# Weight rounding: the sign bit is taken from ScalarE's scaled copy in PSUM instead of from the loaded words

## Chip, cores and metric

The kernel runs on one core of a Trainium2 chip. The metric is the time of one execution on the device in microseconds (us), the median of several runs; lower is better. Times inside an execution come from the hardware profiler's trace of one run.

## What is computed

The reference is a recurrent attention block (RWKV5) followed by a gated feed-forward block (SwiGLU). For 4 batches, 8 heads, 768 time steps and a head dimension of 48 it computes

```
for t in range(S):
    y[t]  = r[t] @ (state + (u * k[t]) v[t]^T)
    state = w * state + k[t] v[t]^T
x   = y as (3072, 384)
g   = x @ w_gate                      # (384, 1536)
out = (silu(g) * (x @ w_val)) @ w_out # (1536, 384)
```

The inputs r, k, v, w and u are 32-bit floats. The three weight matrices arrive as **64-bit floats**: they are drawn as 32-bit numbers and multiplied by a 64-bit scale. [...] the kernel has to round each weight to 32 bits on the chip, and it does so with integer operations. That rounding is where the change lies.

## The kernel before

**Tiling.** Time is cut in chunks of 128 steps, so there are 24 items (6 chunks times 4 batches). For each item the kernel loads r, k and v, scales them by powers of w, transposes them, forms a masked 128x128 score matrix for each head, multiplies it with v, adds what the carried state gives, and updates the state. The result lies transposed in a ring buffer `xT`, ready as an operand of the feed-forward block. That block takes items in pairs: `gate_value` (from L444) multiplies `xT` with 128 columns of w_gate and of w_val into one PSUM bank (L450), ScalarE takes the sigmoid (L456), and VectorE makes two products (L457, L458); L458 is the last reader of the bank. There are two such banks. Later pairs of items run through a faster matrix scheme (L627 and around) whose sums of weights GpSimd makes.

**Weights.** The weights are cut in 18 chunks, each 128 partitions x 768 64-bit words: 6 of w_gate, 6 of w_val (alternating), then 6 of w_out. SyncE's queue issues the loads (L152) into a ring of three slots, `w_bits`, 768 KB each. A word has a low and an upper half of 32 bits. The steps for one chunk `n`, in the order in which `round_act` (from L201) issues them:

1. `round_high(n, 0, 0)`, ScalarE, L173: the upper words of the first half of the chunk (384 of each partition), read as 32-bit floats, are multiplied by 2^-112 into a PSUM tile `w_mag`. The scale turns the exponent of the 64-bit format into that of the 32-bit one, three places too far to the right.
2. `round_low(n)`, ScalarE, L179: the low words, read as unsigned integers and scaled by 2^-29, are rounded to an integer and put in an SBUF tile `w_low` (two slots).
3. `round_dve(n, 0)`, VectorE: L188 takes the sign bit into the weight tile (`wg`, `wv` or `wo`), L189 shifts `w_mag` left by three places and joins it to that sign.
4. `round_high(n, 1, 1)` and `round_dve(n, 1)`: the same for the second half, with `w_mag` in another bank.
5. The load of a further chunk.

In a later turn GpSimd adds `w_low` to the weight tile (`round_pool`, L218; for the first two chunks in halves, L199). The PSUM tile of each half has one buffer only, so the next chunk's L173 of that half waits until L189 has read the last one. Each w_low slot is free again when GpSimd's addition has read it.

**Order.** The schedule is written by hand: every engine executes its instructions in the order in which the program issues them, and semaphores make it wait for the other engines. `gaps` (from L703) and the table `EARLY` put the rounding of three chunks into each step of the attention loop, between its transposes (L343), scores (L381, copied under a mask by VectorE in L386), outputs (L411) and state updates (L426, L438), and pieces of the feed-forward block. ScalarE also makes diagonal matrices (L322) and copies transposed tiles out of PSUM (L347); GpSimd also scales k and r (L301, L304) and makes the products for the diagonal (L230, L231), which VectorE sums (L236). The loads of k, r and v (L115, L121) stand in the same SyncE queue as those of the weights.

Of the kernel before, what the change touches and what calls it, by code (L numbers as in the profile page):

```python
# [9 lines left out]
FP32 = mybir.dt.float32  # L10
INT32 = mybir.dt.int32
UINT32 = mybir.dt.uint32
AF = mybir.ActivationFunctionType
ALU = mybir.AluOpType
# [8 lines left out]
def fast(  # L23
# [44 lines left out]
    dve, pool, act, pe, sp = nc.vector, nc.gpsimd, nc.scalar, nc.tensor, nc.sync  # L68
# [70 lines left out]
    bits, mags, lows = {}, {}, {}  # L139
# [21 lines left out]
    def halves(x, n):  # L161

        c = chunks[n][1].shape[1]
        x = x.rearrange("p (c f) -> p c f", c=c)
        f = x.shape[2]
        return [x[:, :, 0 : f // 2], x[:, :, f // 2 : f]] if c == 3 else [x[:, 0:1], x[:, 1:2]]

    def round_high(n, half, bank):
        hi = halves(bits[n][:, :, 1], n)[half]
        ps, tag = ((ps_w, "w_mag"), (ps_o, "o"))[bank]  # L170
        mag = ps.tile([P, WN // 2], INT32, name="w_mag", tag=tag)
        mags[n, half] = mag[:].rearrange("p (c f) -> p c f", c=hi.shape[1])
        act.activation(  # L173
            mags[n, half].bitcast(FP32), hi.bitcast(FP32), AF.Abs, scale=float(2.0**-112)
        )

    def round_low(n):
# [3 lines left out]
        )  # L181

    def round_dve(n, half):
        hi = halves(bits[n][:, :, 1], n)[half]
        f = hi.shape[2]
        dst = chunks[n][1].bitcast(INT32)
        dst = dst[:, :, half * f : half * f + f] if hi.shape[1] == 3 else dst[:, half : half + 1]
        dve.tensor_scalar(dst, hi, -(1 << 31), None, ALU.bitwise_and)  # L188
        dve.scalar_tensor_tensor(  # L189
            dst, mags.pop((n, half)), 3, dst, ALU.logical_shift_left, ALU.bitwise_or  # L190
        )

    def add_low(n, half):

# [6 lines left out]
    def round_act(next_load=1):  # L201
        n = next_chunk("act")
        if n is not None:
            round_high(n, 0, 0)
            round_low(n)
            round_dve(n, 0)
            round_high(n, 1, 1)
            round_dve(n, 1)
            del bits[n]
            for _ in range(next_load):  # L210
                load_weights()
# [67 lines left out]
    for l in range(7):  # L279
        n = 1 << l  # L280
# [463 lines left out]
    own_sum(1)  # L744
    diagonal(1)
    round_high(0, 0, 0)
    round_low(0)
    flush()
    round_dve(0, 0)
    scores(1)  # L750
    warm(2)
# [514 lines left out]
```

## Time and profile before

| | |
|---|---|
| time, median of 3 runs | 629.39 us (628.95 to 630.25) |
| profiled run: span | 627.9 us |
| TensorE matmul busy | 611.4 us (97%) |
| VectorE busy | 366.8 us (58%) |
| GpSimd busy | 300.1 us (48%) |
| ScalarE busy | 239.5 us (38%) |
| L188, 36 instructions, from 15.4 to 104.4 us | 28.0 us |
| L189, 36 instructions | 20.1 us |
| L173, 36 instructions | 18.9 us |
| L179, 18 instructions | 16.5 us |

How to read the views that follow: a group of instructions is named by its source line, engine and operation, with "output<-inputs" by the names of the program's tiles and their shapes (partitions x elements). After the bar come the busy time in us and the mean duration in ns; after a second bar the time that the engine sat idle just before these instructions, with the instructions that ended most of that idle time ("<-"). A line of the timeline has the start in us, the duration in us (from the first start to the last end where several are merged, "x8"), the instruction, and in brackets an idle time ahead of it. PE is TensorE, DVE is VectorE, ACT is ScalarE, POOL is GpSimd and SP is SyncE. Busy time of TensorE is modelled from pipelined matmuls, so its share of 97% is an upper figure; what counts for this case is where its instructions do not follow one another at once.

### The profile page before, as it was taken

Reading aid. Unit: us, or ns where it says so; the run is one execution under the profiler, and the core shown is the slowest. Engines: PE = TensorE matmul, PEld = TensorE weight load, DVE = VectorE, ACT = ScalarE, POOL = GpSimd, SP = SyncE. Lnnn points to the kernel's source line nnn. Section 1 sums busy time; section 2 is a strip of 40 time slices with the busy share of each in tenths; the row PEclk is TensorE's granted clock in tenths of the full one; section 3 lists DMA queues with packets and bytes.
Section 4 is the critical chain, followed back from the end, with each engine's and each line's share of the span. In section 5 each row is a group of like instructions: output and inputs, shape, how many; then the busy total and the mean of one; then the engine's idle time right before and its main releaser. Section 6 shows DMA issues by size and latency. Waiting matters only on the chain.

```text
span 627.9 us, 13037 instructions
## 1 busy us (share of the span) xinstructions
PE 611.4 (97%) x5040; PEld 550.5 (88%) x5040; DVE 366.8 (58%) x751; ACT 239.5 (38%) x647; POOL 300.1 (48%) x350
## 2 busy tenths in 40 slices
PE   8799999999999999999999999999999999999996
PEld 7588778899888899988899888899988899988896
DVE  6889999465556563466566355665345453355460
ACT  3368777321353512245330435432253321233310
POOL 5789778946648413563543635441433211443110
PEclk9999999999999999999999999999999999999999
DMA  8979873244341203322222402121000000000001
GB/s 191 246 169 243 219 242 94 40 72 80 73 69 24 45 12 66 76 47 45 40 37 57 92 12 37 25 42 41 27 2 1 1 1 26 27 0 1 1 2 55
DMA packets 138007, 40.47 MB, mean 64 GB/s; under 512 B 128592, under 2 KB 131792, under 8 KB 137936
## 3 DMA queue, kind: packets, MB, share of 16 engines
q1 hardware_dynamic: 134480, 34.82, 26.5%
q10 hardware_dynamic: 3456, 4.72, 2.1%
q8 instruction: 42, 0.69, 0.5%
q14 instruction: 29, 0.24, 0.1%
HBM read 28.51 MB, written 4.72 MB: 53 GB/s over the span
## 4 chain that ended last, share of the span: by engine, by line
PE 86%; DVE 7%; ACT 2%; DMA 2%; issue 1%; POOL 0%; DVEq 0%; ACTq 0%; POOLq 0%
PE c_b L627 25%; PE c_a L627 21%; PE o_f L521 13%; PE o_a L521 8%; PE o_b L521 6%; PE y_ps L411 5%; PE gv L450 4%; PE s_ps L381 3%; DVE At L386 1%; PE warm L265 1%; DMA hats<-in_r_dram 1%; DMA w_bits<-in_moe_w_out_dram 1%; DVE wg L188 1%; DVE wo L188 1%; PE u_ps L426 1%
## 5 line engine op out<-in xcount | busy, mean ns | idle before, releaser
L611 POOL TENSOR_TENSOR hT<-hT,u 128x256 f32<-128x256 f32 x60 | 46.9, 782 | 149.0 <-DVE hT L610 121.8
L634 ACT COPY u<-c_a 128x256 f32<-128x256 f32 x120 | 44.5, 371 | 85.8 <-PE c_a L627 83.5
L627 PE MATMUL c_a<-t,wv 128*128 128x256 f32 x240 | 72.0, 382 | 0.1
L627 PE MATMUL c_b<-xT,wg 128*128 128x256 f32 x240 | 71.6, 380 | 0.0
L607 ACT ACTIVATE sg<-hT 128x256 f32<-128x256 f32 x120 | 50.1, 417 | 52.5 <-DVE hT L636 33.8
L322 ACT ACTIVATE At<-ident,du 128x128 f32<-128x128 f32 x176 | 62.1, 398 | 16.2 <-DVE du L236 7.3
L627 PE MATMUL c_b<-xT,s 128*128 128x256 f32 x240 | 61.6, 379 | 0.0
L641 DVE TENSOR_TENSOR u<-u,c_b 128x256 f32<-128x256 f32 x60 | 25.1, 418 | 60.5 <-PE c_b L627 55.4
L627 PEld LDWEIGHTS c_b<-xT,s 128*128 128x128 f32 x240 | 45.2, 190 | 6.6 <-DVE u L641 0.2
L627 PEld LDWEIGHTS c_a<-t,wv 128*128 128x128 f32 x240 | 44.9, 190 | 6.9 <-ACT u L634 1.1
L627 PEld LDWEIGHTS c_b<-xT,wg 128*128 128x128 f32 x240 | 45.3, 190 | 6.0
L636 DVE TENSOR_TENSOR hT<-p,c_b 128x256 f32<-128x256 f32 x60 | 25.1, 419 | 41.6 <-PE c_b L627 38.6
L587 POOL TENSOR_TENSOR s<-wv,wg 128x256 f32<-128x256 f32 x24 | 17.6, 733 | 65.5 <-PE o_f L521 50.8
L386 DVE COPY_PREDICATED At<-mask,s_ps 128x512 f32<-128x512 int32 x48 | 32.9, 741 | 19.9 <-PE s_ps L381 12.4
L450 PE MATMUL gv<-xT,wg 128*128 128x256 f32 x144 | 36.9, 392 | 3.1 <-DVE hT L458 2.5
L304 POOL TENSOR_TENSOR hats<-r_ld,rscale 128x384 f32<-128x384 f32 x20 | 20.9, 1045 | 36.1 <-DMA v_ld<-in_v_dram 19.0
L639 DVE TENSOR_TENSOR hT<-hT,c_a 128x256 f32<-128x256 f32 x60 | 25.3, 421 | 19.8 <-PE c_a L627 18.4
L643 DVE TENSOR_TENSOR hT<-u,c_b 128x256 f32<-128x256 f32 x60 | 25.2, 421 | 19.8 <-PE c_b L627 19.6
L627 PE MATMUL c_b<-t,s 128*128 128x256 f32 x120 | 36.2, 383 | 0.3 <-DVE hT L636 0.3
L411 PE MATMUL y_ps<-At,v_ld 128*32 128x128 f32 x768 | 34.9, 273 | 1.4 <-DVE At L386 1.4
L627 PE MATMUL c_b<-xT,wv 128*128 128x256 f32 x120 | 35.9, 381 | 0.0
L627 PE MATMUL c_a<-t,s 128*128 128x256 f32 x120 | 35.8, 380 | 0.0
(135 smaller groups left out, 1394.6 us busy)
## 6 DMA issues: line engine op xcount, KB each, us to landing
hats<-hats SPq DMA_DIRECT2D x192, 32.0 KB, 2.0
w_bits<-in_moe_w_gate_dram SPq DMA_DIRECT2D x6, 768.0 KB, 6.5
v_ld<-in_v_dram SPq DMA_DIRECT2D x48, 96.0 KB, 3.4
w_bits<-in_moe_w_val_dram SPq DMA_DIRECT2D x6, 768.0 KB, 5.9
w_bits<-in_moe_w_out_dram SPq DMA_DIRECT2D x6, 768.0 KB, 6.0
out_dram<-o_sb ACTq DMA_DIRECT2D x24, 192.0 KB, 1.9
k_ld<-in_k_dram SPq DMA_DIRECT2D x20, 192.0 KB, 3.1
r_ld<-in_r_dram SPq DMA_DIRECT2D x20, 192.0 KB, 3.9
```

Of the source, the lines that this page charges most:

```text
L322: lambda h=h: act.activation(At[i % 2][:, h, :], ident[:], AF.Identity, scale=du[:, h : h + 1])
L386: dve.copy_predicated(At[i % 2][:].rearrange("p (a e) t -> p a e t", e=2)[:, :, e], mask[:].bitcast(INT32).unsqueeze(1).to_broadcast([P, H ...
L411: pe.matmul(ps[32 * q : 32 * q + 32, cc, :], *x, start=start, stop=stop, skip_group_check=True,)
L450: pe.matmul(gv[:, o, :].rearrange("p (i t) -> p i t", i=2), wt[:, c, P * f : P * (f + 1)], xT[:, 2 * g % NX : 2 * g % NX + 2, c, :], start ...
L521: pe.matmul(ps, lhs[:, f, :], rhs[:, f, :], start=(f == 0 and n in (0, 1, 4)), stop=(f == FH - 1), skip_group_check=True,)
L607: act.activation(x[what, f][:], h[j], AF.Sigmoid)
L611: pool.tensor_mul(h[1], h[1], x.pop(("u3", f))[:])
L627: pe.matmul(ps.rearrange("p (i t) -> p i t", i=2), lhs, rhs, start=first, stop=what not in ("p2", "p5", "p4", "p3"), skip_group_check=True,)
L634: act.copy(x[nm, f][:], ps)
L636: dve.tensor_add(h[0], x.pop(("p1", f))[:], ps)
L639: dve.tensor_mul(h[0], h[0], ps)
L643: dve.tensor_add(h[1], x.pop(("u2", f))[:], ps)
```

## The change

ScalarE's function in L173 becomes Copy in place of Abs, so that `w_mag` keeps the sign of the word. VectorE's L188 takes the sign bit out of `w_mag` in PSUM, where it read the loaded words in SBUF. L189 is the same operation as before, on the same operands: the shift by three places drops the sign bit of `w_mag`. The number and the order of instructions on every engine stay the same. What changes besides are the waits: L188 now waits for ScalarE's copy, L189 only for L188, and a slot of `w_bits` no longer has VectorE among its readers.

```
@@ round_high
         act.activation(
-            mags[n, half].bitcast(FP32), hi.bitcast(FP32), AF.Abs, scale=float(2.0**-112)
+            mags[n, half].bitcast(FP32), hi.bitcast(FP32), AF.Copy, scale=float(2.0**-112)
         )
@@ round_dve
-        hi = halves(bits[n][:, :, 1], n)[half]
+        hi = mags.pop((n, half))
         f = hi.shape[2]
         dst = chunks[n][1].bitcast(INT32)
         dst = dst[:, :, half * f : half * f + f] if hi.shape[1] == 3 else dst[:, half : half + 1]
         dve.tensor_scalar(dst, hi, -(1 << 31), None, ALU.bitwise_and)
-        dve.scalar_tensor_tensor(
-            dst, mags.pop((n, half)), 3, dst, ALU.logical_shift_left, ALU.bitwise_or
-        )
+        dve.scalar_tensor_tensor(dst, hi, 3, dst, ALU.logical_shift_left, ALU.bitwise_or)
```

## The prediction

> **What bounds the kernel now.** I read the page's busy shares first (TensorE 97%), then busy time by stage, because the edit lives only where weights are rounded, the first 105 us:
>
> ```profile
> 12.00:40.00 28.00, 23.68 (x384) 18.93 (x383) 23.84 (x43) 14.17 (x34) 21.37 (x22) 1.00 0.91 218
> 40.00:59.00 19.00, 17.97 (x126) 15.30 (x128) 16.24 (x32) 14.39 (x34) 17.74 (x15) 1.00 1.00 235
> 59.00:105.30 46.30, 43.83 (x551) 37.39 (x544) 43.30 (x82) 35.07 (x84) 37.10 (x32) 1.00 0.74 207
> 105.30:627.90 522.60, 516.77 (x3929) 469.69 (x3927) 276.52 (x576) 172.91 (x492) 218.52 (x269) 1.00 0.18 35
> ```
>
> Columns: stretch and length in us; busy us of TensorE, its weight load, VectorE, ScalarE and GpSimd (instructions behind each); granted clock; DMA share; GB/s. From 59 to 105 VectorE is busy 43.30 of 46.30 us and TensorE has 46.30 - 43.83 = 2.47 us of holes. After 105 TensorE is full and nothing of the edit runs there. So the most that can be won is the holes before 105. The timeline of TensorE has the four that lie after 40 us, each with its wait and releaser in brackets:
>
> ```profile
> 58.66 0.43 PE L411 MATMUL y_ps<-rT,Z 112*32 112x128 f32 x8 [1.03 <-ACT kT L347]
> ...
> 76.66 1.53 PE L450 MATMUL gv<-xT,wg 128*128 128x256 f32 x6 [0.98 <-DVE hT L458]
> ...
> 90.12 1.53 PE L450 MATMUL gv<-xT,wg 128*128 128x256 f32 x6 [1.08 <-DVE hT L458]
> ...
> 102.92 1.53 PE L450 MATMUL gv<-xT,wg 128*128 128x256 f32 x6 [0.41 <-DVE hT L458]
> ```
>
> Together 3.50 us. Three of them wait for VectorE's L458, which frees a gate/value bank, and between them TensorE's matmuls follow one another with no gap. VectorE's queue ahead of L458 holds the rounding. Groups by form (busy us, mean ns, then idle before):
>
> ```profile
> L173 ACT ACTIVATE w_mag<-w_bits 128x384 f32<-128x384 f32 x36 | 18.9, 527 | 7.6 <-DVE wg L189 4.0 <-DVE wo L189 1.4 <-DMA w_bits<-in_moe_w_out_dram 1.2
> L179 ACT ACTIVATE w_low<-w_bits 128x768 int32<-128x768 uint32 x18 | 16.5, 917 | 5.1 <-POOL wo L218 3.1 <-POOL wv L218 1.8
> L188 DVE TENSOR_SCALAR wg<-w_bits 128x384 int32<-128x384 int32 x12 | 9.7, 811 | 0.0
> L188 DVE TENSOR_SCALAR wo<-w_bits 128x384 int32<-128x384 int32 x12 | 9.3, 777 | 0.0
> L188 DVE TENSOR_SCALAR wv<-w_bits 128x384 int32<-128x384 int32 x12 | 9.0, 752 | 0.0
> L189 DVE SCALAR_TENSOR_TENSOR wg<-w_mag,wg 128x384 int32<-128x384 int32 x12 | 6.7, 558 | 1.4 <-ACT w_mag L173 0.3
> ```
>
> The reader is to see that L188 is simpler than L189, over the same 384 elements, and yet costs more on average. The view of that line gives its durations as 348 ns at least and 1964 ns at most; L189 stays within 556 to 560. One case from the timelines of VectorE and GpSimd (start, duration) shows what stretches it:
>
> ```profile
> 62.30 1.82 POOL L218 TENSOR_TENSOR wv<-wv,w_low 128x768 int32<-128x768 int32 x1
> ...
> 62.45 1.96 DVE L188 TENSOR_SCALAR wg<-w_bits 128x384 int32<-128x384 int32 x1
> 64.51 0.56 DVE L189 SCALAR_TENSOR_TENSOR wg<-w_mag,wg 128x384 int32<-128x384 int32 x1
> 64.99 0.42 DVE L188 TENSOR_SCALAR wg<-w_bits 128x384 int32<-128x384 int32 x1
> ```
>
> L188 starts just after a GpSimd addition and ends 0.29 us after it (64.41 against 64.12); the next one, with GpSimd idle, takes 0.42.
>
> **What the Trainium skill says.** "VectorE: DVE Perf Modes", section "Why PSUM operands drop a tier": a one-source fp32-sized operation can use both SBUF read ports, but not with a PSUM operand. The trace agrees: 384 elements in 348 ns is under one cycle each at the 0.96 GHz that the page gives. "SBUF — State Buffer", section "Who interferes with whom": an operation in that two-port mode and a GpSimd instruction exclude each other for a whole instruction; one with at most one SBUF input outside that mode does not contend. L188 against L189 (one PSUM, one SBUF input) shows just this. "ScalarE: Activation LUTs", section "Step-by-step: what each stage is for": throughput does not depend on the function; "Table sets: the hidden batching unit" counts abs and copy among what every set holds. L179 is already such a Copy between the same neighbours, and the one table load of ScalarE's timeline up to 106 us is at 0.80.
>
> **The change, part by part.**
>
> *ScalarE, Abs to Copy.* 36 instructions. L179 and L173 fit one line: (917 - 527) / (768 - 384) = 1.016 ns per element, so a Copy of 384 would be 917 - 390 = 527 ns, what Abs takes. Price 0; bounds -0.02 to +0.02 us each, in both directions, since those are the scatter of L173 (495 to 573).
>
> *L188 reads PSUM.* 36 instructions, now 9.7 + 9.3 + 9.0 = 28.0 us. The trace has no one-source form of this size from PSUM. Neighbours: L189 at 558 ns from above (one operand more, same output); from below the first page's table in the section on the errata, (120 + 384) / 0.96 = 525 ns, an estimate. I take 550: 19.8 us, so VectorE has 8.2 us less. With 525 to 558 it is 9.1 to 7.9. A single L188 that met no GpSimd work becomes slower, 0.35-0.44 to 0.55.
>
> *L188 waits for ScalarE.* It stood ahead of the wait for the magnitude, which was L189's, and now stands behind it; VectorE's queue behind it (L189, then L457 and L458, which TensorE waits for) waits too. In 35 of 36 cases the ScalarE copy of the same words had ended before L188 even started, so no wait exists now. The exception is the piece at 19.37: its copy ends about 20.0, so L188 and L189 end 0.65 us later, with the next longer pair 0.8 us, in front of 0.85 us in which VectorE idles at 23.66 anyway: 0. At 87.41 L189 idled 0.46 us; the profile names an L173 ending at 87.09, though that of its own words ended at 84.76. If such a wait came to stand ahead of L188 it would cost up to 0.65 us, in a queue that is 3.9 us ahead by then (below).
>
> *Loads.* A slot of the loaded words is freed by ScalarE alone. The DMA queue's waits put 9.9 + 3.6 + 3.5 = 17.0 us in 5 waits on L188; the load ends earlier where that was the last reader, at 35.30 by about 1 us (L188 ended 35.24, the ScalarE copy 34.27). The k, r and v loads behind it in SP's queue move with it. No TensorE hole after 40 waits for a DMA: 0, never a loss.
>
> *GpSimd.* Without the exclusion its instructions also lose their stretching: additions L218 between 1.81 and 2.02.
>
> Now the four holes.
>
> Hole 1 (58.66) is behind ScalarE's copy of kT, at the end of a ScalarE run with no gap since the L179 at 55.48, which waited for the GpSimd addition ending 55.45. GpSimd is full from 35.98, where it had waited for L189 (end 35.90). The two pairs ahead of that take 2.60 us now (33.30 to 35.90) and 0.55+0.10+0.47+0.55+0.10+0.56 = 2.33 after (0.10 and 0.47 are the start distances of the trace): 0.27. The GpSimd instructions of that run exceed the shortest of their form by some 0.3 in sum. So 0.3 to 0.6; I take **0.5**.
>
> Holes 2 to 4: VectorE runs without idle from 59 to 87. Its L188s from 62.45 to the hole at 76.66 that stand ahead of L458 (six) take 1.96+0.42+0.42+1.26+1.13+0.50 = 5.69, after 6 x 0.55 = 3.30: 2.39 us earlier, against 0.5 + 0.98 = 1.48 needed. Six more up to 90.12 take 1.02+0.41+0.35+1.33+1.20+0.50 = 4.81: 1.51 more, 3.90 in all against 2.56 needed. Six more up to 102.92 take 4.49: 1.19 more, 5.09 against 2.97. All three close: **0.98 + 1.08 + 0.41 = 2.47**. What else must come earlier does: GpSimd's chain there starts at 66.40 after waiting 2.27 us for VectorE, and its end sets L179 and the k and r loads with the weight loads behind them.
>
> Sum: 0.5 + 2.47 = 2.97, less 0.1 for hand-overs: 2.9 us of 627.9. This span is the profiled run's; the timed median is 629.39 (628.95 to 630.25). So 629.39 - 2.9 = **626.5**, -0.46%.
>
> **Rivals.**
> - *More comes out (625.2).* The holes of TensorE before 40 us that wait for engines (1.35 at 17.4, 0.46 at 28.3, 0.60 at 35.5) shrink by half too, 1.3 us more. For it: VectorE and GpSimd are freer there. Against: the first waits for a GpSimd instruction that L188 doesn't meet, and two more holes there wait for DMA.
> - *The relief is soaked up (628.6).* ScalarE's L179 waits 5.1 us in all, almost all for GpSimd, and DMA is at 1.00 of its share from 40 to 59. If these hold the pace, only hole 1 closes by 0.3 and another half: 0.8. For it: L179 waits 1.44 and 1.57 in each stage. Against: those additions start behind GpSimd's wait for VectorE.
> - *Slower (about 634).* VectorE runs ahead until L188 meets ScalarE each time: second halves come behind L179 (0.92 us). The saving per L188 is 28.0/36 - 0.55 = 0.23, per chunk 0.46; if every chunk from 59 on (10) waits 0.92, VectorE loses 10 x 0.46 = 4.6 us in a stretch with no slack. It decides from 0.46 us of wait per chunk. Against: ScalarE is busy only 35.07 of 46.30 there, and was ahead of L188 in every case after 40.
> - *The change doesn't do what it says*: L188 stays stretched by GpSimd because its output still goes to SBUF. L189 has the same output and never is; I give it no share of its own beyond the soaked-up case.
>
> **How the numbers follow.** Chances: forecast 0.56, more 0.19, soaked up 0.19, slower 0.06. The forecast's own range is 625.6 to 627.6 (525 to 558 ns, 0.3 to 0.6 in hole 1, one hole reopening). For 8 in 10 I reach from 624.8 to 628.8, which leaves out the slower case and the edges of the others. About 0.2% (1.26 us) is what a measurement of this kernel can tell from no change: faster by more gets 0.56 + 0.19 + 0.04 of the soaked-up case = 0.79, within 0.15, slower 0.06.
>
> **What would show it.** L188 at 520 to 560 ns with hardly any scatter, beside any GpSimd instruction; L173 unchanged near 527; VectorE with several us of idle between 59 and 105, put down to TensorE or ScalarE; the waits of L450 for L458 gone; the stretch from 105 on of equal length. I am wrong if L188 stays above 0.6 us, if VectorE's new idle is put down to L173 and the holes for L458 stay, or if the holes close and new ones open after 105.

## The result, and the profile after

| | before | after |
|---|---|---|
| time, median (range) | 629.24 us (628.95 to 630.25, 6 runs) | 625.38 us (624.92 to 626.1, 6 runs) |
| ratio, 95% interval | | 0.9938 (0.9925 to 0.9951) |
| span of the profiled run | 627.9 us | 623.3 us |
| L188, 36 instructions | 28.0 us, 348 to 1964 ns | 19.8 us, 535 to 558 ns |

The kernel is 3.9 us (0.62%) faster; 2.9 us were forecast. At 625.38 us it lies 0.2 us below the range that the prediction gives the forecast itself (625.6 to 627.6) and inside the wider one (624.8 to 628.8). In the tables of the kernel after, lines from L190 on have numbers lower by two than before (L448 is the L450 of before, L456 its L458, L216 its L218).

Busy time by stage of the kernel after, columns as before, from 59 us on:

```profile
59.00:103.00 44.00, 44.00 (x536) 38.33 (x529) 39.59 (x84) 35.37 (x86) 37.11 (x34) 1.00 0.73 208
103.00:623.30 520.30, 514.88 (x3914) 468.92 (x3910) 273.22 (x570) 171.38 (x488) 214.15 (x266) 1.00 0.18 35
```

TensorE is busy 44.00 of 44.00 us from 59 to 103, and VectorE now idles 44.00 - 39.59 = 4.41 us there: the engine that had no slack has some, and TensorE has none. TensorE's timeline of the kernel after at the four places, with the group (71.93) ahead of the second:

```profile
57.76 0.43 PE L409 MATMUL y_ps<-rT,Z 112*32 112x128 f32 x8 [0.29 <-ACT kT L345]
...
71.93 1.56 PE L448 MATMUL gv<-xT,wg 128*128 128x256 f32 x6
...
74.62 1.46 PE L448 MATMUL gv<-xT,wg 128*128 128x256 f32 x6
...
86.77 1.46 PE L448 MATMUL gv<-xT,wg 128*128 128x256 f32 x6
...
98.91 1.46 PE L448 MATMUL gv<-xT,wg 128*128 128x256 f32 x6
```

Three holes are gone (no bracket), the first has 0.29 us left. The view brackets only idle times of 0.15 us and more. The rounding's groups by form after:

```profile
L173 ACT ACTIVATE w_mag<-w_bits 128x384 f32<-128x384 f32 x36 | 18.9, 526 | 2.2 <-DVE wg L189 1.0 <-DVE hT L456 0.8 <-DVE Z L436 0.4
L179 ACT ACTIVATE w_low<-w_bits 128x768 int32<-128x768 uint32 x18 | 16.5, 918 | 5.0 <-POOL wv L216 2.9 <-POOL wo L216 2.1
...
L189 DVE SCALAR_TENSOR_TENSOR wg<-w_mag,wg 128x384 int32<-128x384 int32 x12 | 6.7, 558 | 0.4
...
L188 DVE TENSOR_SCALAR wo<-w_mag 128x384 int32<-128x384 int32 x12 | 6.6, 554 | 1.3 <-ACT w_mag L173 1.0
L188 DVE TENSOR_SCALAR wv<-w_mag 128x384 int32<-128x384 int32 x12 | 6.6, 550 | 1.2 <-ACT w_mag L173 1.2
L188 DVE TENSOR_SCALAR wg<-w_mag 128x384 int32<-128x384 int32 x12 | 6.6, 548 | 1.1 <-ACT w_mag L173 1.1
```

L188 has lost its scatter, L189 is as it was, Copy costs what Abs did (526 against 527 ns). New is the wait of L188 for L173.

**Where the time came from.** Mark in both timelines where the score matmuls (s_ps) of each item start and subtract:

| s_ps before (us) | after minus before | hole passed since the row above, as listed | closed |
|---|---|---|---|
| 53.68 | -0.16 | | |
| 66.93 | -0.90 | 1.03, 0.29 left | 0.74 |
| 80.29 | -2.11 | 0.98 | 1.21 |
| 93.75 | -3.43 | 1.08 | 1.32 |
| 106.55 | -4.08 | 0.41 | 0.65 |
| 182.76 | -4.08 | | |

So between 53.68 and 182.76 us the 3.92 us come from the four holes and nowhere else. Each of the three holes that closed fully gave 0.23 to 0.24 us more than its listed idle time. The kernel before shows why, with the group ahead of the second hole:

```profile
72.82 1.56 PE L450 MATMUL gv<-xT,wg 128*128 128x256 f32 x6
```

From there to the 76.66 of the hole are 3.84 us; after, 71.93 to 74.62 are 2.69. The difference is 1.15, where the hole is listed as 0.98: in these dense rows a matmul group starts before the modelled end of the one ahead (the group between, from 73.33, is listed for 1.46 us, to 74.79, and the next starts at 74.62), and listed idle time counts only from that end. The remaining 0.06 or so lie behind the hole (76.66 to 80.29 is 3.63 us, 74.62 to 78.18 is 3.56).

The profiled spans differ by 4.6 us, 0.5 more than the table's 4.08. Of that, 0.42 lie between the starts at 182.76 and 220.31, where the run of before has one more hole (0.29 us, near 196), far behind the rounding. It comes and goes: the first experiment, which keeps the slow L188, has none there, and the kernel with the first twelve chunks has one of 0.35 us at 190.31. So it is not counted as an effect of the change.

### The profile page after: what moved, and what is told of

Its sections match the earlier page's. It is cut to its first block, busy times and chain, and to the rows that moved or that the text cites. A ratio compares the mean times of both kernels' runs of the same rounds, so it can differ in the third digit from the quotient of the medians.

```text
span 623.3 us, 13014 instructions
## 1 busy us (share of the span) xinstructions
PE 611.0 (98%) x5040; PEld 552.1 (89%) x5040; DVE 358.6 (58%) x751; ACT 238.9 (38%) x647; POOL 296.9 (48%) x350
## 4 chain that ended last, share of the span: by engine, by line
PE 90%; POOL 2%; DMA 1%; ACT 1%; DVE 1%; issue 0%; SPq 0%; ACTq 0%; POOLq 0%
PE c_b L625 25%; PE c_a L625 21%; PE o_f L519 13%; PE o_a L519 8%; PE gv L448 7%; PE o_b L519 6%; PE y_ps L409 5%; PE s_ps L379 3%; PE u_ps L424 1%; PE tp L341 1%; DMA r_ld<-in_r_dram 1%; POOL wg L216 1%; POOL wv L216 1%; POOL rk L228 0%; POOL hats L299 0%
## 5 line engine op out<-in xcount | busy, mean ns | idle before, releaser
L448 PE MATMUL gv<-xT,wg 128*128 128x256 f32 x144 | 36.7, 391 | 0.6 <-ACT xT L413 0.6
```

Source lines behind the costliest of these rows:

```text
L448: pe.matmul(gv[:, o, :].rearrange("p (i t) -> p i t", i=2), wt[:, c, P * f : P * (f + 1)], xT[:, 2 * g % NX : 2 * g % NX + 2, c, :], start ...
```

## The experiments

Times stand beside the kernel before, run on the same chip: 629.45 us beside the first four, 629.63 beside the next four, 630.04 beside the two after those and 629.66 beside the last two. The change itself gave 625.67 and 625.27 us beside the second four and the last. "Copy alone" and the exchange of operations are edits of the kernel before, all others of the change. Where an edit adds lines, the numbers behind them are higher; the tile names tell which operation it is.

**Copy alone.**

```diff
-            mags[n, half].bitcast(FP32), hi.bitcast(FP32), AF.Abs, scale=float(2.0**-112)
+            mags[n, half].bitcast(FP32), hi.bitcast(FP32), AF.Copy, scale=float(2.0**-112)
```

> Abs becomes Copy, but L188 goes on taking the sign from the loaded words in SBUF. Theory (ScalarE's function costs nothing, the whole gain is VectorE's L188): 629.2 us within 0.4, L173 at 527 ns. Rival (Copy itself is faster or moves ScalarE): 1 us or more below, L173 under 500 ns.

Measured: 629.79 us, ratio 1.0003 (0.9994 to 1.0012); L173 at 525 ns, L188 as before. ScalarE's function alone is worth nothing that this can show, so the gain lies with VectorE's L188 and what it reads.

**Only the first twelve chunks, only the last six.**

```diff
-        hi = mags.pop((n, half))
+        mag = mags.pop((n, half))
+        hi = mag if n < 12 else halves(bits[n][:, :, 1], n)[half]
...
-        dve.scalar_tensor_tensor(dst, hi, 3, dst, ALU.logical_shift_left, ALU.bitwise_or)
+        dve.scalar_tensor_tensor(dst, mag, 3, dst, ALU.logical_shift_left, ALU.bitwise_or)
```

In the second kernel the condition is `n >= 12`. In both, the sign operation is L189 and the joining one L190.

> The sign comes from PSUM for chunks 0 to 11 only (w_gate, w_val); the six chunks of w_out take it from the loaded words. Theory (VectorE gains a lead that it keeps): at the end of chunk 11 VectorE was about 3.0 us ahead of the kernel before, so the holes of TensorE close up to 3.0 us in sum and the rest stays open ahead of 100 us: 626.3 us (625.8 to 626.9). Rival (each hole closes only by what its own chunks save): the first two holes close, the last two stay, 627.1 us or more.

> The reverse: the sign comes from PSUM for chunks 12 to 17 only (w_out). Theory: the holes at 58.66 and 76.66 stay, those at 90.12 and 102.92 close by about 1.2 and 0.65 us: 627.4 us (626.9 to 628.0). The gains of the two halves add up to more than the 3.9 us of both, since a lead from the first also closes the later holes. Rival (GpSimd and ScalarE hold the later stages): 628.5 us or more.

Measured: 625.66 us (ratio 0.9936, 0.992 to 0.9953) and 628.18 us (0.9977, 0.9969 to 0.9985). The first twelve chunks alone give 3.8 us, all that can be told apart from the change itself, although w_out's sign operation still meets GpSimd. Its group in that kernel, and the only idle time of TensorE listed between 40 and 105 us there:

```profile
L189 DVE TENSOR_SCALAR wo<-w_bits 128x384 int32<-128x384 int32 x12 | 9.6, 801 | 0.1
```

```profile
57.96 0.42 PE L410 MATMUL y_ps<-rT,Z 112*32 112x128 f32 x8 [0.31 <-ACT kT L346]
```

So a lead won early pays for slow instructions later. It lasts just to the end: at the place of the fourth hole TensorE idles 0.11 us (at 99.38, too short for the view), and between the two s_ps starts around it (90.52 and 103.01) it takes 12.49 us where the change takes 12.15. I had put the lead at 3.0 us, too low; a likely reason, not tested, is that VectorE idles in the change, so that its time there doesn't show all it could be ahead. The last six alone leave the first two holes and close the others, as expected:

```profile
59.01 0.43 PE L410 MATMUL y_ps<-rT,Z 112*32 112x128 f32 x8 [1.03 <-ACT kT L346]
...
77.00 1.53 PE L449 MATMUL gv<-xT,wg 128*128 128x256 f32 x6 [0.97 <-DVE hT L457]
```

Its time fell by 1.3 us, less than the 2.0 I expected; the s_ps starts moved by 1.87 us between 66.93 and 106.55, but lay 0.35 late ahead of that. The two parts add up to 3.8 + 1.3 = 5.1 us, more than the 3.9 of both. By their intervals the times alone leave this open; the traces show it, since the third hole and most of the fourth close in each of the two kernels: gains don't add where a lead is carried on.

**The two operations change places.**

```diff
-        dve.tensor_scalar(dst, hi, -(1 << 31), None, ALU.bitwise_and)
-        dve.scalar_tensor_tensor(
-            dst, mags.pop((n, half)), 3, dst, ALU.logical_shift_left, ALU.bitwise_or
-        )
+        dve.tensor_scalar(dst, mags.pop((n, half)), 3, None, ALU.logical_shift_left)
+        dve.scalar_tensor_tensor(dst, hi, -(1 << 31), dst, ALU.bitwise_and, ALU.bitwise_or)
```

> Abs as before, but the two VectorE operations change places: L188 shifts the magnitude out of PSUM (one source, no wait less than in the change), L189 takes the sign from the loaded words and joins it (two SBUF inputs). Theory (the cost was the meeting with GpSimd on SBUF, and it goes where two SBUF ports are used): L188 at 550 ns without scatter, L189 scattered from 0.56 to 1.9 us and above 0.85 in the mean, VectorE some 3 us longer from 59 to 105, time about 631 (629.5 to 633). Rival (reading PSUM in the first operation is what gains): L189 stays at 558 ns, time 625 to 627.

Measured: 631.53 us, ratio 1.0032 (1.002 to 1.0045), as expected. Its groups by form, and one meeting with GpSimd on the timeline:

```profile
L189 DVE SCALAR_TENSOR_TENSOR wv<-w_bits,wv 128x384 int32<-128x384 int32 x12 | 12.7, 1055 | 0.4
L189 DVE SCALAR_TENSOR_TENSOR wg<-w_bits,wg 128x384 int32<-128x384 int32 x12 | 10.5, 871 | 0.4
...
L188 DVE TENSOR_SCALAR wg<-w_mag 128x384 int32<-128x384 int32 x12 | 6.6, 548 | 1.1 <-ACT w_mag L173 1.1
```

```profile
64.09 1.84 POOL L216 TENSOR_TENSOR wv<-wv,w_low 128x768 int32<-128x768 int32 x1
...
64.40 0.55 DVE L188 TENSOR_SCALAR wg<-w_mag 128x384 int32<-128x384 int32 x1
...
64.98 1.36 DVE L189 SCALAR_TENSOR_TENSOR wg<-w_bits,wg 128x384 int32<-128x384 int32 x1
```

This settles what is gained. The first operation reads PSUM here too, at 548 ns, and runs through the middle of a GpSimd addition untouched. The second has two SBUF inputs now, ends 0.41 us after that addition (66.34 against 65.93) and takes 0.87 to 1.06 us in the mean, with single ones from 557 to 1889 ns. In the kernel before the operation in its place, with one input in PSUM and one in SBUF, took 556 to 560 ns. The stretching went to the operation with the second SBUF input, and the time with it: TensorE's holes for L456 (the L458 of before) are 1.00, 1.18 and 1.19 us at 78.18, 91.74 and 105.32, and there is a new one of 1.43 us at 52.02. The rival, that reading PSUM in the first operation is what pays, falls.

**Low words last on ScalarE.**

```diff
             round_high(n, 0, 0)
-            round_low(n)
             round_dve(n, 0)
             round_high(n, 1, 1)
             round_dve(n, 1)
+            round_low(n)
```

> The change, with ScalarE's order within a chunk turned from upper half, low words, upper half to both upper halves and then the low words, so that the second L188 no longer stands behind a copy of low words (L179) that waits for GpSimd. Theory (TensorE sets the pace from 58 us on, VectorE's new waits for ScalarE cost nothing): the 3.2 us that VectorE waits for L173 shrink to about 1, the time stays at 625.4 within 0.6. Rival (the new wait is what is left to gain): 624.4 or less.

> The change itself, run beside the next three: 625.4 us within 0.6.

Measured: 625.45 us against 625.67 of the change beside it. VectorE's wait for L173 fell from 3.2 us (in 6 waits) only to 2.5 (in 3), so the edit did less than I meant, and nothing of it after 59 us (two waits of 1.43 us in all, where the change has four of 1.31). The time stayed. That the change's new wait costs nothing after 59 us is told better by TensorE's row in the change, which has no hole there. Ahead of 59 us the wait of 0.82 us at 56.10 is gone with this edit, and the hole at 57.85 is no smaller (0.46 us).

**The sign operation twice in first halves.**

```diff
-        dve.tensor_scalar(dst, hi, -(1 << 31), None, ALU.bitwise_and)
+        for _ in range(2 - half):
+            dve.tensor_scalar(dst, hi, -(1 << 31), None, ALU.bitwise_and)
```

> The change, with L188 done twice in the first half of each chunk (same result): 18 x 0.58 = 10.4 us more work for VectorE, 5.8 of it after 59 us. Theory (VectorE has 1 to 2 us of slack at each place where TensorE waits for L456, so only the part beyond it shows): by 86 us six chunks have added 3.5 us, some 1.2 of it in former idle time, against 1.0 of slack: 1.3 us of hole there and little after it, 627.0 us (626.2 to 628.2). Rival (VectorE still sets the pace): 630 us or more.

Measured: 628.27 us (627.63 to 631.46 in 20 executions), just outside what I expected, and about midway between the 627.0 expected and the rival's 630. TensorE's holes for VectorE after 40 us:

```profile
50.62 1.53 PE L449 MATMUL gv<-xT,wg 128*128 128x256 f32 x6 [0.43 <-DVE hT L457]
...
88.18 1.53 PE L449 MATMUL gv<-xT,wg 128*128 128x256 f32 x6 [0.56 <-DVE hT L457]
...
101.13 1.53 PE L449 MATMUL gv<-xT,wg 128*128 128x256 f32 x6 [0.56 <-DVE hT L457]
```

Of 10.4 us of extra VectorE work, 2.6 show in the times. The trace is of the fastest of the 20 executions. In it the s_ps starts fall behind those of the change run beside it by 0.67, 0.79 and 0.80 us at these three holes, 2.26 in all, where 0.43 + 0.56 + 0.56 = 1.55 are listed: the price of a hole found above, once more. I had not seen the one at 50.62, and had priced a hole at its listed idle time.

**What holds the last hole.** Four kernels went after the 0.3 us at 57.8. The first puts off every copy of low words, with the load issued behind it, to the next gap of the attention loop; the second only chunk 7's, again with its load; the third joins that to "low words last". The fourth leaves order and loads alone and gives every third chunk another place for its low words:

```diff
-        lows[n] = two.tile([P, WN], INT32, name="w_low", tag="w_low")
+        if n % 3 == 2:
+            lows[n] = wt[2].rearrange("p f n -> p (f n)")[:, 0:WN].bitcast(INT32)
+        else:
+            lows[n] = two.tile([P, WN], INT32, name="w_low", tag="w_low")
```

The core of the second, chunk 7 alone, where `flush_low` runs at the start of the next gap:

```diff
-            round_low(n)
+            if n != 7:
+                round_low(n)
             round_dve(n, 0)
             round_high(n, 1, 1)
             round_dve(n, 1)
+            if n == 7:
+                held_low.append((n, next_load))
+                return
...
+    def flush_low():
+        while held_low:
+            n, next_load = held_low.pop(0)
+            round_low(n)
+            del bits[n]
+            for _ in range(next_load):
+                load_weights()
```

> The change, with the copy of the low words (L179), and the next load behind it, put off to the beginning of the next gap of the attention loop, which is behind the copies of the transposed tiles (kT, rT). Theory (the last hole of the 40 to 105 us stretch, 0.29 us before the first y_ps of item 4, is held by an L179 that waits for GpSimd ahead of the kT copy): that hole closes, 0.29 + 0.24 = 0.5 us, 624.9 us (624.3 to 625.4). Rival (loads that come later, or GpSimd waiting for low words, cost more than that): 625.6 or more, with a wait of TensorE or GpSimd for w_low or of ScalarE for w_bits.

> The change, with only chunk 7's copy of the low words (and the load behind it) put off past the kT and rT copies of item 4; all other chunks as in the change. Theory (the late loads were what cost when all were put off; the hole of 0.29 to 0.4 us at 57.8 us is held by this one copy): that hole closes, no wait for w_bits comes in its place, 0.5 us less, 625.1 us (624.6 to 625.5). Rival (the hole is held by something else, or chunk 10's later load opens another): 625.5 or more, with a wait for w_bits or a hole for L456 near 67 us.

> The same with the low words last in every other chunk too. Theory: as the kernel with chunk 7 alone put off, 625.1 us within 0.5, since VectorE's waits for ScalarE cost nothing here. Rival: 0.5 us or more below it.

> The change, with a third place for the low words: every third chunk's copy (L179) goes to a weight tile that is not yet in use (wt), so that the copy of chunk 7 waits for the addition of chunk 4 and not of chunk 5. Loads stay where they are. Theory (the remaining hole at 57.8 us is this copy's wait for GpSimd, and earlier trials lost it to late loads only): that hole of 0.3 to 0.4 us closes with no other in its place, 0.5 us under the change measured beside it; ScalarE's wait of L179 for GpSimd falls from 5.0 us to under 1. Rival (another engine takes its place): same time as the change within 0.2 us.

> The change itself beside the kernel with three places for low words: 625.5 us within 0.5.

Measured: 637.79, 627.14 (ratio 0.9957, 0.9945 to 0.997), 626.98 (0.9955, 0.9943 to 0.9968) and 625.84 us, the last beside 625.27 of the change. All four miss what I expected, and none beats the change. The third is no different from the second, so the order of ScalarE's copies shows no worth here either. With chunk 7 put off, the hole at 57.8 is gone, but ScalarE's and then TensorE's timeline show what it cost:

```profile
57.76 0.93 ACT L179 ACTIVATE w_low<-w_bits 128x768 int32<-128x768 uint32 x1
...
67.04 0.52 ACT L173 ACTIVATE w_mag<-w_bits 128x384 f32<-128x384 f32 x1 [2.57 <-DMA w_bits<-in_moe_w_val_dram]
```

```profile
76.05 1.53 PE L462 MATMUL gv<-xT,wg 128*128 128x256 f32 x6 [0.67 <-DVE hT L470]
```

The load of w_val behind it was issued at 61.44 instead of 53.76 us; L188 then waits 1.90 us for that L173, and the hole comes back at 76.05. It was chunk 9's load, not chunk 10's as I had written: its slot was free, and only its place in the program held it. A version that puts off the copy and leaves the load was not tried. With all copies put off ScalarE waits for loads five times after 40 us, at most 3.84, 6.54 and 4.90 us.

With a third place for the low words, L179 no longer waits for GpSimd at all, and TensorE's hole is still there. Timelines of ScalarE, VectorE and TensorE in that kernel, where L192 is the joining operation:

```profile
55.45 0.52 ACT L173 ACTIVATE w_mag<-w_bits 128x384 f32<-128x384 f32 x1 [2.06 <-DVE wg L192]
```

```profile
53.81 0.56 DVE L192 SCALAR_TENSOR_TENSOR wg<-w_mag,wg 128x384 int32<-128x384 int32 x1
```

```profile
58.91 0.42 PE L412 MATMUL y_ps<-rT,Z 112*32 112x128 f32 x8 [0.30 <-ACT kT L348]
```

The view puts ScalarE's wait down to VectorE, but that does not fit. This L173 is the first half of chunk 7, and the L192 that frees its PSUM tile is the one above, which ended at 54.37, 1.08 us before the L173 started. (In the profile of the change L173 followed that operation by 0.03 us, at 53.20.) What came just before 55.45 is the load of chunk 7's own words: issued at 48.43, it landed at 55.36 by the trace's record of its completion. The first repeat of the change shows the same: L173 starts at 54.64, the load had landed at 54.56, L179 does not wait for GpSimd there either, and the hole is 0.36 us, while in the two other profiles of the change L179 waits 1.00 us for GpSimd. In the kernel with the first twelve chunks the view names the load itself:

```profile
53.59 0.53 ACT L173 ACTIVATE w_mag<-w_bits 128x384 f32<-128x384 f32 x1 [1.17 <-DMA w_bits<-in_moe_w_val_dram]
```

So two things stand close behind each other at this place, GpSimd's addition and the load of chunk 7, and which of them comes last changes between executions of one and the same kernel. Removing one of them gave nothing here. Whether the third place would close the hole in an execution where the load is in time is not shown.

## Why the prediction was right, point by point

- **What bounds.** Right: after 40 us VectorE, stretched by GpSimd, held TensorE only through the four holes; the s_ps starts at 106.55 and 182.76 moved by the same 4.08 us.
- **Copy costs what Abs does.** Right, as "Copy alone" shows (525 ns). The sum for it was empty: the line through 917 and 527 ns gives back the 527 that it was drawn through, and the bounds of 0.02 us are narrower than the scatter named for them (495 to 573 ns).
- **L188 at 550 ns, 19.8 us.** Measured 548 to 554 in the mean, 6.6 + 6.6 + 6.6 = 19.8 us. GpSimd's additions lost their stretching too: 1.82 to 1.85 us, where they were 1.82 to 2.02. The exchange of places shows the stretching on an operation with two SBUF inputs and not on one that reads PSUM alone, as the Trainium skill has it ("SBUF — State Buffer", section "Who interferes with whom"). One saving was not in the sum: L189 now starts 0.03 us after the end of L188, where it was 0.10, some 36 x 0.07 = 2.5 us more for VectorE by this estimate. L189 had a wait of its own before and has none now, and L188 reads PSUM now; the runs don't tell which of the two does it.
- **Holes 2 to 4 close.** Right, in the step where savings are added up from 59 us on: the L458 that each hole waited for starts 3.77, 4.20 and 5.33 us earlier, where 2.39, 3.90 and 5.09 were worked out. The first-twelve kernel shows that the lead of the first chunks carries to the end but for 0.11 us of idle time.
- **Hole 1, taken as 0.5.** 0.74 closed, more than the 0.3 to 0.6 allowed; the path was right and its first two terms were too small. VectorE's two pairs took 2.18 us (33.26 to 35.44), not the 2.33 worked out, since the 0.10 us between L188 and L189 were carried over from the trace of before: 0.42 less than the 2.60 of before, not 0.27. GpSimd started 0.39 us earlier (35.59 against 35.98; VectorE was there 0.04 earlier, and the hand-over took 0.07 longer), and its run from there to the end of the addition that L179 waits for took 19.10 us against 19.47, so 0.37 of stretching went where I had 0.3. L179 then started 0.75 us earlier and ScalarE's way from it to the matmul at the hole was 0.15 shorter; TensorE itself was there 0.16 earlier, which leaves 0.74.
- **The sum, 2.97 less 0.1.** This is the term that was mis-sized most. The listed idle times of holes 2 to 4 were added as they stand, 2.47 us, and they gave 1.21 + 1.32 + 0.65 = 3.18: a closed hole was worth its listed idle time plus about 0.24 us. The 0.1 taken off for hand-overs had the wrong sign. With 0.74 for hole 1 this makes 3.92.
- **L188 waits for ScalarE: nearly nothing.** The price is right, the reason only in part. I counted the copies that were done in time in the old order of events; once VectorE was ahead, six waits of 3.2 us in all appeared. After 59 us they fall in slack, as TensorE's 44.00 of 44.00 us show. The slower rival named this mechanism; the four waits after 59 us come to 1.31 us in ten chunks, 0.13 a chunk, where it decides from 0.46.
- **Loads.** The load expected about 1 us earlier was issued at 34.23 instead of 35.30. The experiments with late loads show that later ones are a loss. No run has the earlier loads alone; that they give nothing is argued from the traces, where no hole after 40 us waits for a load in the kernel before.
- **More comes out.** That rival's 625.2 us is nearer to the measured 625.38 than the forecast's 626.5, but not for its reason. It named the holes ahead of 40 us; those stayed (1.34, 0.40 and 0.60 us, after 1.35, 0.46 and 0.60; at 53.68 the change is 0.16 us ahead). Half of the three would also have been 1.2 us, not 1.3, and not two but three more holes there wait for DMA. The extra came from the price of the holes and from hole 1.
- **L189's idle 0.46 us at 87.41** in the kernel before stays unexplained.

## What to carry to other kernels

When a simple instruction scatters, here from 0.35 to 1.96 us, suspect that it meets another engine: look for a GpSimd instruction that ends just before it does, and try an operand in PSUM if one is at hand, though the shortest instructions get slower (0.35 to 0.55 us here). A helper engine's saving is worth only the holes that it closes on the bounding engine: measure them from start to start against a dense row, not by their listed idle time. A lead that is won early can carry over later stages, so try the first stages of an edit alone before doing it everywhere. And where a view names who ended a wait, check that the one named had not long been done.

## What the runs showed of the hardware that I had not expected

A hole ahead of a gate/value group in TensorE's row cost 0.23 to 0.24 us more than its listed idle time, in holes that closed (0.98 listed, 1.21 regained; 1.08 and 1.32; 0.41 and 0.65) and in holes that opened (0.43 listed, 0.67 lost; 0.56 and 0.79; 0.56 and 0.80, with the sign operation done twice).

Where an L188 that reads SBUF meets GpSimd, the start can decide which of the two is held up. In the kernel before three L188s that started 0.02 us ahead of a GpSimd addition (at 67.54, 80.58 and 93.70) took 0.42, 0.35 and 0.35 us, as with GpSimd idle (0.42 at 64.99, 0.35 at 91.22), and the additions behind them took 1.95, 2.02 and 2.02 us, where the shortest took 1.82. The L188 at 62.45, which started 0.15 us behind an addition, took 1.96 us.

In the kernel with all copies of low words put off, TensorE was busy only 3.25 of 6 us from 90 to 96, and the clock granted from 96 to 105 was 0.62, where it is 1.00 in that stretch of the other kernels. Its s_ps starts fall 3.0 us further behind those of the change there (96.84 against 90.32, then 112.00 against 102.47), a part of the 12 us that it is slower. What lowers the clock was not tested.
